# Splitting the first batch's input loads between two issuing engines in an attention and two-MoE kernel

## The chip, the cores and the metric

The kernel runs on one core of a Trainium2 chip. The metric is the device time of one execution in microseconds (us), the median of several runs. One core has five engines with instruction streams of their own: TensorE (PE, matrix multiplications), VectorE (DVE), ScalarE (ACT, activation functions and copies), GpSimd (POOL) and SyncE (SP, which here only issues transfers). Transfers between device memory (HBM) and the on-chip memory (SBUF) are moved by 16 DMA engines, which the issuing engines share. An engine carries out its instructions in program order; a transfer is also an instruction of the engine that issues it, and the instruction waits until the semaphores it names have reached their values.

## The reference, cut to what matters

Three layers in a row. The first is an attention over 32 memory slots per head, for 4 batches of 8 heads and 576 positions with a head size of 64; its output (2304 tokens of 512 numbers) goes through a gated feed-forward layer of 1536, and then through 8 experts of 1024 of which each token takes the best two.

```python
a = softmax(phi, axis=2)                       # phi (4, 8, 576, 32)
k_m = einsum('bhsm,bhsd->bhmd', a, k)          # 32 memory keys per head
v_m = einsum('bhsm,bhsd->bhmd', a, v)
attn = softmax(q @ k_m.T / 8) @ v_m            # (4, 8, 576, 64)
x = attn, heads joined                         # (2304, 512)
x = (silu(x @ w_gate) * (x @ w_val)) @ w_out   # 512 -> 1536 -> 512
logits = x @ g + log1p(exp(x @ n)) * noise     # 8 experts, best two
out = sum over the two of weight * (relu(x @ w1[e]) @ w2[e])
```

## The kernel before

The tokens are worked in 8 blocks of 288, two blocks to a batch, and the 8 heads of a batch in two groups g = 0, 1 that fill the 128 partitions (four heads of 32 slots for phi, 128 rows of positions for keys and values, two heads of 64 for queries). What the change touches is the start of the program, the work of the first batch ahead of block 0.

**The loads.** All loads of this stretch are issued by SP (`Q` in the code; `A` is ACT). `load_phi(0, 0)` and `load_phi(0, 1)` come first (128 partitions by 576 numbers each, 288 KB), then `load_part(0, 0, 0)` (the keys of group 0), `load_q(0)` (the queries of block 0), and the keys of group 1, the values of group 0 and the values of group 1 (each 128 by 1152 numbers, 576 KB). Behind them `load_wa` loads pieces of the first layer's weights, 512 KB each, 16 at once and later ones as `low` frees the places (tiles stg, early, stw, stx).

**The waits of a transfer.** Each transfer that SP or ACT issues signals one of eight semaphores (DMAHW0 to DMAHW7) when it has landed, and these are given out in turn in the order of the program, over both issuing engines together. A transfer therefore waits, before it is issued, for the landing of the one eight places earlier in the program. The seven input loads and the first weight load take the eight semaphores for the first time and wait for nothing.

**The work of the first batch.** For each group: `s1_a` (the maximum of phi over positions, DVE), `s1_e` (the exponential, ACT), `s1_b` (transposes, PE), `s1_bc` (their copy out, ACT, tile en), then `s1_c` (the product with keys or values, PE, tile pkv), `s1_cv`, `s1_d` and `s1_dc` (scaling, transposing and copying into tile km). `s2_first` and `s2_a`, `s2_e`, `s2_b`, `s2_c`, `s2_d` are the scores and the second softmax of block 0 (tiles psc, sm, at, x). `proj_a` multiplies the memory values into the first layer's weights, and `gv(0, f)` are block 0's gate products for the slice f of 1536/12 (tiles pg, pv), `down(0, f)` its output product (tile acc). Before its first exponential ACT loads its function table (line 232, by a first activation on a small tile named warm). `spin(n)` is n matmuls of ones, whose result nobody reads. `top` (ACT) and `low` (DVE) turn each loaded weight piece into 32-bit numbers; `low` frees its place. The queries of block 1 (`load_q(1)`) are issued in block 0's slice 3; their first reader on PE are the score products of block 1 (line 343, tile psc).

Each engine's order is that of these calls, written out by hand; nothing reorders it.

Of the kernel before, what the change touches and what calls it, by code (L numbers as in the profile page):

```python
# [74 lines left out]
def moe_program(ctx, tc, xin, wa, wgn, nz, wb, out):  # L75
# [10 lines left out]
    V, A, P, G, Q = nc.vector, nc.scalar, nc.tensor, nc.gpsimd, nc.sync  # L86
# [28 lines left out]
    PH, KV, QT, RA = {}, {}, {}, {}  # L115
    ROW = 18 * D

    def section(b, name):
        o, n = PLACE[name]
        return xin[b, o:o + 128 * n].rearrange("(p n) -> p n", n=n)  # L120

    def load_phi(b, g):
        t = att.tile([128, S], F32, tag="phi", name="phi", bufs=2)
        Q.dma_start(t, section(b, f"phi{g}"))
        PH[b, g] = t

    def load_part(b, g, s):
        if (b, g) not in KV:
            if b == 0 and g:
                KV[b, g] = wpool.tile([128, 4096], F32, tag="X1", name="kv", bufs=1)[:, :2 * ROW].rearrange(  # L130
                    "p (s w) -> p s w", s=2)
            else:
                KV[b, g] = att.tile([128, 2, ROW], F32, tag="kv", name="kv", bufs=1)
        Q.dma_start(KV[b, g][:, s], section(b, f"{'kv'[s]}{g}"))

    def load_kv(b, g):
        for s in range(2):
            load_part(b, g, s)

    def load_q(i):  # L140
        QT[i] = att.tile([128, 4, BT], F32, tag="q", name="qt", bufs=1)
        Q.dma_start(QT[i], section(i // 2, f"q{i % 2}").rearrange("p (q t) -> p q t", q=4))

    ORDER = [(0, 0), (0, 1), (1, 0), (1, 1)]
    for f in range(NF1):
# [59 lines left out]
    def low(n):  # L205
# [3 lines left out]
        for m in FREES.get(n, ()):  # L209
            load_wa(m)  # L210

    load_phi(0, 0)
    load_phi(0, 1)
    load_part(0, 0, 0)
    load_q(0)
    for g, s in ((1, 0), (0, 1), (1, 1)):
        load_part(0, g, s)
# [500 lines left out]
    for b in range(1, B):  # L718
        i = 2 * b - 2
        n = AT["s1"][min(b, 2)]  # L720
        for g in range(2):
            later(i, 18.5 if b == 1 else -4, load_phi, b, g)
        later(i, 18.5 if b == 1 else -4, load_kv, b, 0)
        later(i, n[5] + 0.06, load_kv, b, 1)
        later(i, n[0], both, s1_a, b)
        later(i, n[1], both, s1_e, b)
        later(i, n[2], both, s1_r, b)
        for g in range(2):
            for m, fn in zip(n[3 + 6 * g:], (s1_b, s1_bc, s1_c, s1_cv, s1_d, s1_dc)):
                later(i, m, fn, b, g)  # L730
        for j, o in enumerate(AT["proj"][b]):
            i, f = 2 * b - 1 + o // NF1, o % NF1
            put(i, 2 * f + 1.95, proj_a, b, j)
            later(i, 2 * f + 2, proj_h, b, j)
            later(i, 2 * f + 2, proj_b, b, j)
    for i in range(1, NB):
        put(i - 1, 6, load_q, i)
        n = AT["s2"].get(i - 1, AT["s2"][2])
        put(i - 1, n[0], s2_p, i)
        put(i - 1, n[1], s2_t, i)  # L740
        put(i - 1, n[2], both, s2_a, i)
        put(i - 1, n[3], both, s2_e, i)
        for g in range(2):
            for m, fn in zip(((n[4], n[5], n[6]), (n[7], n[8], n[9]))[g], (s2_b, s2_c, s2_d)):
                put(i - 1, m, fn, i, g)
# [594 lines left out]
    for p in range(pairs):  # L1340
        e, q = 2 + p // 4, p % 4
# [62 lines left out]
    for p in range(pairs):  # L1404
        e, q = 2 + p // 4, p % 4
# [135 lines left out]
```

## Time and profile before

| | |
|---|---|
| median of 3 runs | 840.27 us (839.26 to 840.96) |
| the profiled execution | 842.7 us, of which the span shown by the profile is 840.9 us |
| PE busy | 824.5 us, 98% of the span |
| DVE, ACT, POOL busy | 636.9, 391.0, 243.8 us |
| moved by DMA | 143.20 MB, 170 GB/s over the span |

Times of rows count from the start of the span. The 1.8 us between the span and the execution's time lie outside the instructions shown. A busy PE is not a PE at its peak, since matmuls overlap and their ends are modelled. PE's busy digit is 7 in the first of the profile's 40 slices (21 us each), 6 in the last and 9 in all others, so the places where PE could be waited out are at the two ends.

### The profile page before, as it was taken

The numbers are of one execution on the slowest core, as the hardware profiler recorded it, in microseconds if no ns is written. First come the engines' busy times: TensorE is split into PE (matmuls) and PEld (weight loads), VectorE is DVE, ScalarE is ACT, GpSimd is POOL, SyncE is SP. The second block draws the span as 40 slices with busy tenths as digits, with TensorE's granted clock in tenths as the row PEclk, the third lists the DMA queues.
The fourth block names the chain that finished last, engine by engine and source line by source line (L and its number), as shares of the span: only waits on it lengthen the run. The fifth ranks groups of instructions, "written<-read, shape, count | busy, mean of one in ns | idle before, by whom it ended". The sixth has DMA issues, their size and how long they took to land.

```text
span 840.9 us, 16644 instructions
## 1 busy us (share of the span) xinstructions
PE 824.5 (98%) x6317; PEld 731.9 (87%) x6317; DVE 636.9 (76%) x1534; ACT 391.0 (47%) x804; POOL 243.8 (29%) x345
## 2 busy tenths in 40 slices
PE   7999999999999999999999999999999999999996
PEld 5777988899999998999999988988888888888885
DVE  5888588766867677777784587898889988899771
ACT  5765565343433334333444545546445454554430
POOL 2000012524333142444123223322415234144242
PEclk9999999999999999999999999999999999999999
DMA  9994748784427373447946993645574654654421
GB/s 349 401 347 138 227 153 303 243 262 134 116 67 217 86 211 84 134 112 176 269 151 204 222 244 73 137 128 114 129 170 100 160 125 102 164 136 113 161 84 64
DMA packets 79145, 143.20 MB, mean 170 GB/s; under 512 B 16176, under 2 KB 36880, under 8 KB 79056
## 3 DMA queue, kind: packets, MB, share of 16 engines
q1 hardware_dynamic: 59696, 100.66, 39.0%
q0 software_dynamic: 19360, 41.38, 20.8%
q8 instruction: 52, 0.85, 0.4%
q14 instruction: 37, 0.30, 0.1%
HBM read 105.34 MB, written 36.68 MB: 169 GB/s over the span
## 4 chain that ended last, share of the span: by engine, by line
PE 81%; DMA 9%; DVE 5%; issue 2%; ACT 1%; SPq 1%; POOL 1%; POOLq 0%; DVEq 0%; ACTq 0%
PE acc L1177 18%; PE ph L1163 17%; PE acc L496 14%; PE pg L463 9%; PE pv L463 7%; PE ph L974 4%; PE acc L992 3%; PE pp L343 2%; DMA wb<-wb 2%; PE acc L492 1%; DMA stx<-wa 1%; DMA out<-pv,ix 1%; DMA kv<-xin 1%; PE pT L518 1%; DMA qt<-xin 1%
## 5 line engine op out<-in xcount | busy, mean ns | idle before, releaser
L1177 PE MATMUL acc<-ws,hs 128*128 128x512 f32 (+1 forms) x690 | 174.9, 394 | 0.0
L1163 PEld LDWEIGHTS ph<-xh,ws 128*128 128x128 f32 x1008 | 151.0, 188 | 9.7 <-ACT y L1200 0.7
L1163 PE MATMUL ph<-xh,ws 128*128 128x308 f32 x1008 | 157.4, 304 | 0.3 <-ACT y L1200 0.3
L1177 PEld LDWEIGHTS acc<-ws,hs 128*128 128x128 f32 (+1 forms) x690 | 122.7, 184 | 24.3
L496 PE MATMUL acc<-a,ro 128*128 128x288 f32 x576 | 116.4, 295 | 0.0
L1017 POOL DMA_INDIRECT out<-pv,ix x40 | 63.1, 1576 | 175.2 <-ACT pv L1009 66.9
L496 PE MATMUL acc<-a,os 128*128 128x288 f32 x432 | 105.8, 294 | 0.0
L463 PE MATMUL pg<-x,pt 128*128 128x288 f32 x576 | 102.3, 311 | 1.9 <-DVE ta L476 0.9
L463 PEld LDWEIGHTS pg<-x,pt 128*128 128x128 f32 x576 | 81.1, 188 | 20.4 <-issue 6.0
L496 PEld LDWEIGHTS acc<-a,ro 128*128 128x128 f32 x576 | 92.2, 188 | 0.0
L463 PE MATMUL pv<-x,pt 128*128 128x288 f32 x576 | 91.9, 295 | 0.0
L463 PEld LDWEIGHTS pv<-x,pt 128*128 128x128 f32 x576 | 81.7, 188 | 0.0
L476 DVE SCALAR_TENSOR_TENSOR ta<-ta,pg 128x288 f32<-128x288 f32 x84 | 37.8, 450 | 57.4 <-ACT ta L471 57.3
L660 POOL DMA_INDIRECT xs<-R,gidx x48 | 47.0, 979 | 110.5 <-DMA xs<-R,gidx 94.3
L496 PEld LDWEIGHTS acc<-a,os 128*128 128x128 f32 x432 | 74.1, 189 | 0.1
L471 ACT ACTIVATE ta<-pg 128x288 f32<-128x288 f32 x84 | 34.3, 408 | 79.7 <-PE pg L463 79.7
L482 ACT ACTIVATE a<-ta 128x288 fp32r<-128x288 f32 x84 | 37.3, 444 | 71.9 <-DVE ta L477 71.7
L453 POOL DMA_DIRECT2D os<-osl x72 | 40.8, 567 | 100.7 <-PE acc L496 58.5
L974 PE MATMUL ph<-xt,wm 128*128 128x384 f32 (+1 forms) x256 | 55.4, 307 | 0.0
L974 PEld LDWEIGHTS ph<-xt,wm 128*128 128x128 f32 x256 | 43.7, 189 | 2.5
L477 DVE TENSOR_TENSOR ta<-ta,pv 128x288 f32<-128x288 f32 x84 | 38.1, 454 | 8.7
L483 DVE TENSOR_TENSOR a<-ta,a 128x288 fp32r<-128x288 f32 x84 | 37.4, 445 | 5.2 <-ACT a L482 4.9
(241 smaller groups left out, 1449.9 us busy)
## 6 DMA issues: line engine op xcount, KB each, us to landing
wb<-wb SPq DMA_DIRECT2D x70, 512.0 KB, 4.3
os<-osl POOLq DMA_DIRECT2D x72, 256.0 KB, 3.4
kv<-xin SPq DMA_DIRECT2D x16, 576.0 KB, 6.9
xl<-xs SPq DMA_DIRECT2D x40, 160.0 KB, 6.5
stg<-wa SPq DMA_DIRECT2D x12, 511.8 KB, 10.4
out<-zt SPq DMA_DIRECT2D x1, 5888.0 KB, 26.0
xd<-R SPq DMA_DIRECT2D x8, 603.0 KB, 5.6
qt<-xin SPq DMA_DIRECT2D x8, 576.0 KB, 7.4
```

Of the source, the lines that this page charges most:

```text
L453: G.dma_start(r(lo), r(osl[f][:, :]))
L463: P.matmul(p, r(PT[f // 2, g][:, w, f % 2, 128 * a:128 * a + 128]), r(X[i][:, s, g, :]), start=(n == 0), stop=(n == 5))
L476: V.scalar_tensor_tensor(ta, ta, 1.0, pg, op0=OP.add, op1=OP.mult)
L477: V.tensor_mul(ta, ta, pv)
L482: A.activation(r(ah[:, 0, :]), ta, AF.Copy)
L483: V.tensor_sub(r(ah[:, 1, :]), ta, ah[:, 0, :])
L496: P.matmul(ACC[i][c], r(OS[i, f][w][:, o]), r(ah[:, s, :]), start=(f == 0 and n == 0), stop=(f == NF1 - 1 and n == 2))
L660: G.indirect_dma_start(out=xs[:, :], out_offset=bass.IndirectOffsetOnAxis(ap=RT[i][:, t, n:n + 1], axis=0), in_=R[i][:, t, :], in_offset=None)
L974: P.matmul(p, r(w[:, c]), r(x[:, k, b, :]), start=(m == 0), stop=(m == 11))
L1017: G.indirect_dma_start(out=out, out_offset=bass.IndirectOffsetOnAxis(ap=IX[e][:h, t:t + 1], axis=0), in_=PV[e, t][:h], in_offset=None, com ...
L1163: P.matmul(out, r(w[i][:, c + 128 * k:c + 128 * k + 128]), r(x[:, m, k, a]), start=(start and n == 0), stop=(n == 5), skip_group_check=not ...
L1177: P.matmul(AC2[e, t][:h], r(a[:, n, o]), r(w[b][:, n]), start=(f == 0 and m == 0), stop=(f == NF2 - 1 and m == 2))
```

## The change

For batch 0 the keys, the values and the queries are each loaded by two transfers of 64 partitions, the lower half issued by SP and the upper half by ACT; of the two loads of phi, group 0's stays on SP and group 1's goes to ACT. Later batches are loaded as before. There are 12 transfers in the place of 7, the six of ACT standing ahead of its table load.

```diff
+    def halves(two, t, src):
+        if two:
+            Q.dma_start(t[:64], src[:64])
+            A.dma_start(t[64:], src[64:])
+        else:
+            Q.dma_start(t, src)
+
     def load_phi(b, g):
         t = att.tile([128, S], F32, tag="phi", name="phi", bufs=2)
-        Q.dma_start(t, section(b, f"phi{g}"))
+        if b == 0:
+            (A if g else Q).dma_start(t, section(b, f"phi{g}"))
+        else:
+            Q.dma_start(t, section(b, f"phi{g}"))
...
-        Q.dma_start(KV[b, g][:, s], section(b, f"{'kv'[s]}{g}"))
+        halves(b == 0, KV[b, g][:, s], section(b, f"{'kv'[s]}{g}"))
...
-        Q.dma_start(QT[i], section(i // 2, f"q{i % 2}").rearrange("p (q t) -> p q t", q=4))
+        halves(i == 0, QT[i], section(i // 2, f"q{i % 2}").rearrange("p (q t) -> p q t", q=4))
```

SP's first instructions before, with the semaphores each waits for (kv_98 holds keys and values of group 0, kv_102 those of group 1, stg the first weight pieces):

```order
L124 DMA phi_94<-xin 128x576
L124 DMA phi_96<-xin 128x576
L134 DMA kv_98<-xin 128x1152
L142 DMA qt_100<-xin 128x1152
L134 DMA kv_102<-xin 128x1152
L134 DMA kv_98<-xin 128x1152
L134 DMA kv_102<-xin 128x1152
L176 DMA stg_106<-wa 128x2047
L176 DMA stg_108<-wa 128x2047 [waits DMAHW0_49]
L176 DMA stg_110<-wa 128x2047 [waits DMAHW1_49]
L176 DMA stg_112<-wa 128x2047 [waits DMAHW2_49]
```

All input loads are issued without a wait, and the fourth weight load is the one that waits for the keys of group 0 (DMAHW2). The same place on SP now (kv_104 is group 1's tile):

```order
L132 DMA phi_94<-xin 128x576
L124 DMA kv_98<-xin 64x1152
L124 DMA qt_101<-xin 64x1152
L124 DMA kv_104<-xin 64x1152
L124 DMA kv_98<-xin 64x1152 [waits DMAHW0_49]
L124 DMA kv_104<-xin 64x1152 [waits DMAHW2_49]
L186 DMA stg_111<-wa 128x2047 [waits DMAHW4_49]
L186 DMA stg_113<-wa 128x2047 [waits DMAHW5_49]
L186 DMA stg_115<-wa 128x2047 [waits DMAHW6_49]
L186 DMA stg_117<-wa 128x2047 [waits DMAHW7_49]
```

With more transfers in the same round of eight semaphores, the halves of the values wait for landings, and every weight load does. ACT's first instructions before:

```order
L232 ACT_TABLE_LOAD
L232 ACTIVATE warm_143<-warm_143 128x1 [waits Pool_49]
L272 ACTIVATE phi_94,st_170<-phi_94,st_170 128x576 [waits DMAHW0_49,DVE_49]
L272 ACTIVATE phi_96,st_172<-phi_96,st_172 128x576 [waits DMAHW1_49,DVE_49]
L294 ACTIVATE en_219<-pT_211 128x512 [waits PE_49]
```

The table load was the first of them. Now:

```order
L132 DMA phi_96<-xin 128x576
L125 DMA kv_98<-xin 64x1152
L125 DMA qt_101<-xin 64x1152
L125 DMA kv_104<-xin 64x1152
L125 DMA kv_98<-xin 64x1152 [waits DMAHW1_49]
L125 DMA kv_104<-xin 64x1152 [waits DMAHW3_49]
L242 ACT_TABLE_LOAD
L242 ACTIVATE warm_148<-warm_148 128x1 [waits Pool_49]
L282 ACTIVATE phi_94,st_175<-phi_94,st_175 128x576 [waits DMAHW0_49,DVE_49]
L282 ACTIVATE phi_96,st_177<-phi_96,st_177 128x576 [waits DVE_49]
```

Six transfers stand ahead of the table load on ACT. The fifth waits for the landing of phi of group 1 (DMAHW1), the sixth for that of the upper half of the keys of group 0 (DMAHW3, the second row).

## Rows read from the trace of the kernel before

**Rows 1.** The page: PE's busy time, and the DMA share by slice
```profile
PE 824.5 (98%) x6317; PEld 731.9 (87%) x6317; DVE 636.9 (76%) x1534; ACT 391.0 (47%) x804; POOL 243.8 (29%) x345
...
DMA  9994748784427373447946993645574654654421
```

**Rows 2.** Busy time in two stretches: engines, granted clock, DMA share, GB/s
```profile
0.00:5.00 5.00, 3.38 (x30) 3.12 (x30) 1.53 (x4) 1.87 (x3) 4.41 (x17) 1.00 0.59 204
5.00:10.00 5.00, 3.99 (x56) 3.35 (x57) 1.01 (x6) 2.77 (x8) 0.63 (x1) 1.00 0.98 358
```

**Rows 3.** Timeline of SP's transfers: start, us, what
```profile
0.76 0.86 SPq L124 DMA_DIRECT2D phi<-xin  x2
...
8.71 0.33 SPq L176 DMA_DIRECT2D stg<-wa  x1
...
40.80 0.33 SPq L142 DMA_DIRECT2D qt<-xin  x1
```

**Rows 4.** Tiles phi and kv in the first 30 us: issue and landing
```profile
DMA to landing us min/median/max: 3.0/3.2/3.3
...
L134 SPq DMA_DIRECT2D kv<-xin x4: 424/436/1617, 1.7 to 3.6; - x4
...
DMA to landing us min/median/max: 7.0/9.4/10.9
```

**Rows 5.** Timeline of ACT, idle time before and what ended it in brackets
```profile
0.76 1.28 ACT L232 ACT_TABLE_LOAD   x1 [0.76 <-PEq L1533]
...
4.62 0.77 ACT L272 ACTIVATE phi<-phi,st 128x576 f32<-128x576 f32 x1 [2.36 <-DVE st L267]
...
17.04 0.79 ACT L203 ACTIVATE top<-stg 128x512 f16<-128x512 bf16 x1
...
31.32 0.79 ACT L203 ACTIVATE top<-stw 128x512 f16<-128x512 bf16 x1 [1.61 <-DMA stw<-wa]
```

**Rows 6.** Timeline of DVE
```profile
16.46 0.46 DVE L368 TENSOR_TENSOR sm<-sm,rd 128x288 f32<-128x288 f32 x1
...
17.87 0.69 DVE L207 SCALAR_TENSOR_TENSOR wa<-stg,top 128x512 int32<-128x512 int32 x1 [0.35 <-ACT top L203]
...
32.15 0.69 DVE L207 SCALAR_TENSOR_TENSOR wa<-stw,top 128x512 int32<-128x512 int32 x1 [1.07 <-ACT top L203]
```

**Rows 7.** Timeline of PE
```profile
5.54 1.11 PE L285 MATMUL pT<-ident,phi 128*128 128x128 f32 x4 [1.14 <-ACT phi L272]
...
8.83 1.03 PE L307 MATMUL pkv<-kv,en 128*32 128x64 f32 x40 [0.47 <-ACT en L295]
...
28.73 2.21 PE L492 MATMUL acc<-a,ro 128*128 128x288 f32 x8 [0.86 <-DVE ro L207]
...
34.17 1.08 PE L463 MATMUL pg<-x,pt 128*128 128x288 f32 x6
...
35.98 0.66 PE L343 MATMUL pp<-wa,km 64*32 64x256 f32 x16
...
37.39 2.21 PE L492 MATMUL acc<-a,ro 128*128 128x288 f32 x8
...
39.22 0.64 PE L463 MATMUL pg<-x,pt 128*128 128x288 f32 x2
...
41.65 2.10 PE L492 MATMUL acc<-a,ro 128*128 128x288 f32 x8
...
45.26 1.09 PE L343 MATMUL pp<-wa,km 64*32 64x256 f32 x32
46.29 2.21 PE L492 MATMUL acc<-a,ro 128*128 128x288 f32 x8
...
51.19 0.72 PE L343 MATMUL psc<-qt,km 64*32 64x288 f32 x16 [1.11 <-DMA qt<-xin]
...
77.19 0.60 PE L285 MATMUL pT<-ident,phi 128*128 128x128 f32 x4
```

## The prediction

> **What bounds the kernel now.** The page comes first: PE is busy for 824.5 of 840.9 us [rows 1], so a change to the loads of the first batch can move the time only where PE waits near the start. The second view is the busy time by stretch. The DMA engines reach a share of 0.59 in the first 5 us and 0.98 in the next five [rows 2], and the page's DMA digits read 9 for the first three slices, 63 us [rows 1]: from about 5 us on, the transfers run at the rate of the DMA engines and not at that of the engine that issues them. The third view is the timelines of ACT, DVE and PE over the first 55 us. Two things run side by side there. One is a chain of computation: phi lands, its exponential starts on ACT at 4.62 [rows 5], then transposes and the first product with the keys on PE at 8.83 [rows 7], the second softmax on DVE [rows 6], and PE's first output product at 28.73, for which PE waited 0.86 us on DVE [rows 7]. The other is the stream of weight loads, which ACT meets at 31.32, after 1.61 us of idle time that a landing ended [rows 5], and which PE meets at 51.19, where it had waited 1.11 us for the queries of block 1 [rows 7]. So the stream sets the time up to 51.19, and the chain has room against it that I work out below.
>
> **What the change adds and removes on the issue side.** SP has six input transfers in place of seven and ACT six in place of none. A transfer of SP takes 0.42 to 0.44 us of its sequencer, with one of 1.62 [rows 4]. No row shows one on ACT, nor one of 64 partitions: from below it could be nearly free, from above 1.62; I take 0.43, the usual value, as a rate that does not depend on the size of the tile. The bytes stay the same. What an earlier issue can win is time in which the DMA engines stand idle after the first issue: 0.41 of the first 5 us, 2.05 us, less the 0.76 us before any issue [rows 2, 3], so at most 1.3 us.
>
> [...]
>
> **What the change adds on ACT.** The six transfers stand ahead of ACT's table load. Four need no wait; the fifth waits for phi of group 1 and the sixth for the upper half of group 0's keys. ACT goes in order, so behind these two waits stand the table load, both exponentials of phi, and with them the whole chain of computation. Phi landed 3.0 to 3.3 us after its issue [rows 4], near 4 us, so the fifth costs nothing beyond the sixth. The sixth decides. In the kernel before, the fourth weight load waits on the keys of group 0 and starts at 8.71 [rows 3]; that is their landing, and it agrees with 7.0 us, the shortest time from issue to landing of the four [rows 4]. That is the upper end. The lower end is a landing in the order of issue at the rate that the DMA engines ran: phi and these keys are 2 x 288 + 576 KB, 1.18 MB; 204 GB/s over 5 us are 1.02 MB, and the rest at 358 GB/s takes another 0.45 us [rows 2], so 5.5 us. I take 7.6, two thirds of the way to the upper end: that row is the direct one and the same bytes stand ahead, but the issue comes about 0.45 us earlier and less stands behind.
>
> Then ACT issues the last half (0.43), loads its table (1.28 [rows 5]) and runs the small first activation. Before, the table load started at 0.76 and ACT was idle again 2.36 us ahead of 4.62, at 2.26 [rows 5], so both take 1.50 us. The exponential starts at 7.6 + 0.43 + 1.50 and some 0.07 of gaps, 9.6. Against 4.62 that is 5.0 us late; by the ends of the landing 2.9 (exponential at 7.5) and 6.1 (10.7).
>
> **How much of it reaches the end.** Step by step along the chain:
> - PE had waited 0.47 us before the key product at 8.83 [rows 7], just behind the landing at 8.71. Late transposes use that up: minus 0.47.
> - The score products and the value products find their data landed; DVE's second softmax follows at the same distance. At 17.87 DVE had waited 0.35 us for ACT's second `top` [rows 6], which ACT began at 17.04, 0.12 us after DVE had finished its subtraction at 16.92 [rows 5, 6]. With the chain late, both weight pieces have landed and the `top` work is done ahead: minus 0.35. From there to 31 us DVE's row of work has no gap, so the rest passes on in full: 5.0 - 0.82 = 4.2 us at PE's output product of 28.73.
> - From there PE's own waits are waits for the stream. One pair of products before a projection takes 1.81 us (34.17 to 35.98), the next takes 2.43 (39.22 to 41.65): 0.62 lost. One double projection takes 1.41 (35.98 to 37.39), a later one 1.03 (45.26 to 46.29): 0.38 lost. At 51.19 it is 1.11 [rows 7]. Together 2.1 us, which a late PE does not wait. ACT and DVE can fall back on their idle 1.61 and 1.07 us [rows 5, 6] and what follows.
> - The weight loads themselves do not get late with the chain: each waits for a landing eight places earlier, and the places they need had been freed long before. That holds the queries of block 1, issued at 40.80 [rows 3], at their place.
> - After 51.19 PE is at 98% and more and gives nothing back.
>
> So the chain costs 4.2 - 2.1 = 2.1 us; with the ends of the landing 0.0 (2.9 - 0.82 - 2.1) and 3.2. The profiled execution took 842.7 us, a span of 840.9 and 1.8 outside it; the sum against it is 844.8. The median of the runs lies 2.4 us under the profiled execution, and the forecast goes from the median: 840.3 + 2.1 = 842.4. A measurement of this kernel tells about 0.2% from no change, 1.7 us.
>
> **The rivals.**
> First, the stream covers all of it: the keys land near 5.5 us, because in the kernel before it was the transfers queued behind them that held them up, and now fewer stand there. Then the chain is 2.1 us late at 28.73 and the three waits absorb it: no change, between -0.4 and +1.0 us. For it: the rate of the DMA engines allows it. Against it: 7.0 us for the shortest landing.
> Second, and on the other side, the earlier issue leads. Two sequencers fill the DMA engines sooner, every later transfer lands up to 1.3 us earlier, the queries of block 1 with them, and PE's waits at 35 to 51 us shrink. This decides only from the point where ACT is released so early that the chain stays under the waits, with the keys' landing near 5.5: 840.3 - 1.3 = 839.0. For it: 0.59 of share in the first stretch. Against it: the first bytes cannot come sooner than phi's first issue, which stays where it is, and the same late exponential takes away what it wins.
> [...]
> [...]
>
> **How the numbers follow.** The forecast (842.4, own range 841.3 to 843.5, from landings at 6.5 and 8.7) has 0.45; the covered case 0.30; the leading stream 0.08; the clock 0.17. Slower by over 0.2% holds about 0.7 of the forecast and all of the clock case but a little, and a bit of the covered case: 0.51. Within 0.2% is most of the rest, 0.44. Faster by over 0.2% would need more than the 1.3 us that the stream can win: 0.05. The range is 839.6 to 844.8: down into the leading stream's case, up over the clock's.
>
> **What would show it.** Right: ACT's table load starts at 7 to 9 us in place of 0.76, just behind its sixth transfer, and the first exponential between 9 and 10.7; PE's idle time ahead of the transposes is 5 us longer; PE's wait for the queries of block 1 is gone. Wrong: a table load before 6 us (then the landing was the mis-sized term and the time stays); the queries' landing more than 1 us away from 51; idle time of PE at a weight wait after 52 us; or transposes and key products at a different speed than in rows 7.

## The result

The changed kernel is slower: 847.13 us (median of 6 runs, 845.39 to 849.08) against 840.81 for the kernel before (6 runs), a ratio of 1.0076 with an interval of 1.0064 to 1.0087. The forecast had the direction and gave 842.4, with an upper end of 844.8. Five single executions among the runs below took over 1000 us; the ratios and their intervals leave these out, the medians do not.

The profiled execution of the changed kernel took 845.39 us. Its page, the rows that answer to [rows 1] and the span:

```profile
span 843.6 us, 16654 instructions
...
PE 822.9 (98%) x6317; PEld 732.4 (87%) x6317; DVE 636.2 (75%) x1534; ACT 390.5 (46%) x804; POOL 243.7 (29%) x345
...
DMA  9993838884427364447846993645564654654421
```

No engine is busier than before by more than 0.5 us (PEld) and the DMA engines are as busy in the first three slices; the time went into waiting. What ACT did at the start, as [rows 5] (ACTq are the transfers that ACT issues):

```profile
1.21 0.55 ACTq L125 DMA_DIRECT2D kv<-xin  x1
...
2.42 6.32 ACTq L125 DMA_DIRECT2D kv<-xin  x3
8.77 1.28 ACT L242 ACT_TABLE_LOAD   x1 [8.77 <-DMA kv<-xin]
10.06 0.20 ACT L242 ACTIVATE warm<-warm 128x1 f32<-128x1 f32 x1
10.17 0.76 ACT L282 ACTIVATE phi<-phi,st 128x576 f32<-128x576 f32 x1
```

The table load starts at 8.77 in place of 0.76, right behind the sixth transfer, and the exponential at 10.17 in place of 4.62. The busy time by stretch, as [rows 2], with the two stretches that follow (the last two columns are the DMA share and GB/s):

```profile
0.00:5.00 5.00, 3.38 (x30) 3.12 (x30) 0.43 (x3) 0.00 (x0) 4.41 (x17) 1.00 0.62 183
5.00:10.00 5.00, 0.00 (x0) 0.00 (x0) 1.35 (x2) 1.23 (x1) 0.63 (x1) 0.81 1.02 271
10.00:15.00 5.00, 3.92 (x52) 3.33 (x52) 0.63 (x4) 3.30 (x10) 0.00 (x0) 0.51 1.04 259
15.00:20.00 5.00, 4.84 (x129) 2.85 (x125) 2.61 (x8) 2.05 (x5) 0.00 (x0) 1.00 1.02 363
```

This is what the forecast had not seen: from 5 to 15 us the DMA engines have a share of 1.02 and 1.04 and move 271 and 259 GB/s. The first of them had 358 before [rows 2]; the second was this:

```profile
10.00:15.00 5.00, 4.85 (x139) 2.93 (x138) 2.84 (x8) 1.30 (x4) 0.00 (x0) 1.00 1.02 412
```

The engines are full and slow. PE of the changed kernel, as [rows 7]:

```profile
11.07 1.11 PE L295 MATMUL pT<-ident,phi 128*128 128x128 f32 x4 [6.67 <-ACT phi L282]
...
13.83 1.33 PE L317 MATMUL pkv<-kv,en 128*32 128x64 f32 x40
...
33.83 2.21 PE L502 MATMUL acc<-a,ro 128*128 128x288 f32 x8 [0.86 <-DVE ro L217]
...
54.10 0.72 PE L353 MATMUL psc<-qt,km 64*32 64x288 f32 x16
```

PE is 5.1 us late at its first output product (28.73 before) and 2.9 at the score products of block 1 (51.19 before), where it no longer waits for the queries. The key product takes 1.33 us in place of 1.03. Set against the first trace of before, that reads like the forecast. But the median moved by 6.3 us, and these two executions stand only 2.7 us apart: the first trace of before is of an execution 1.9 us over its median, this one is 1.7 us under. The experiments had to find out which of the two comparisons is usual.

### The profile page after: what moved, and what is told of

It is laid out like the page before. It is cut to its first block, busy times and chain, and to the rows that moved or that the text cites. A ratio compares the mean times of both kernels' runs of the same rounds, so it can differ in the third digit from the quotient of the medians.

```text
span 843.6 us, 16654 instructions
## 1 busy us (share of the span) xinstructions
PE 822.9 (98%) x6317; PEld 732.4 (87%) x6317; DVE 636.2 (75%) x1534; ACT 390.5 (46%) x804; POOL 243.7 (29%) x345
## 4 chain that ended last, share of the span: by engine, by line
PE 89%; DVE 5%; DMA 2%; issue 2%; ACT 1%; ACTq 0%; POOL 0%; POOLq 0%; DVEq 0%
PE acc L1187 18%; PE ph L1173 17%; PE acc L506 14%; PE pg L473 9%; PE pv L473 8%; PE acc L1002 7%; PE ph L984 7%; PE acc L502 3%; PE pp L353 3%; PE pkv L317 1%; DMA out<-pv,ix 1%; PE pT L528 1%; DMA kv<-xin 1%; PE psc L353 1%; PE plg L539 1%
```

## The experiments

All times are medians with the ratio to the kernel before, of the same chip and session. A ratio's interval is the 95% one.

| run | us | before | ratio and interval |
|---|---|---|---|
| after_again | 845.96 | 839.98 | 1.0058 (1.0035 to 1.0082) |
| sp_halves | 846.92 | 839.98 | 1.0074 (1.0050 to 1.0097) |
| act_four | 842.69 | 839.98 | 1.0029 (1.0012 to 1.0046) |
| hold | 844.00 | 839.98 | 1.0042 (1.0027 to 1.0057) |
| sp_even_odd | 841.84 | 840.72 | 1.0018 (1.0006 to 1.0030) |
| even_odd | 844.32 | 840.72 | 1.0046 (1.0030 to 1.0062) |
| two_whole | 840.31 | 840.72 | 0.9988 (0.9970 to 1.0006) |
| four_even_odd | 840.62 | 840.13 | 1.0005 (0.9994 to 1.0017) |
| hold_spin | 842.90 | 840.13 | 1.0028 (1.0017 to 1.0039) |
| two_whole_b | 841.43 | 840.13 | 1.0017 (1.0002 to 1.0031) |
| late_values | 846.60 | 840.38 | 1.0075 (1.0063 to 1.0087) |
| after_c | 846.24 | 840.38 | 1.0070 (1.0057 to 1.0082) |
| even_odd_c | 843.55 | 840.38 | 1.0044 (1.0027 to 1.0061) |
| hold_c | 843.78 | 840.38 | 1.0045 (1.0032 to 1.0058) |

**The changed kernel again** (after_again, no edit).

> The changed kernel once more, for a second trace and more times. Three theories of the 6.3 us. Hold: ACT waits for the upper half of group 0's keys, the chain of computation is late, and PE is late by 5 us at its first output product. Stream: the halves on two queues are moved slower (the first trace of the changed kernel has 271 and 259 GB/s from 5 to 15 us, before 358 and 412), so the weights and the queries of block 1 land about 2 us late. Clock: PE's idle 6.7 us ahead of the transposes cost it the full clock for a stretch. All three expect about 847 here. Hold expects the table load near 8.8 again; stream expects the queries of block 1 to be issued near 43 in place of 40.8, later in a slower run; clock expects the low stretch to differ between runs and the slower runs to have the lower mean clock.

845.96. The table load starts at 7.27 here, not near 8.8, and the rates are 259 and 258 GB/s from 5 to 15 us: the slow stream is a property of the kernel and not of one execution. The queries of block 1 are issued at 43.20, as the stream theory expected.

**The halves without the hold** (sp_halves).

```diff
-            A.dma_start(t[64:], src[64:])
+            Q.dma_start(t[64:], src[64:])
...
-            (A if g else Q).dma_start(t, section(b, f"phi{g}"))
+            Q.dma_start(t, section(b, f"phi{g}"))
```

> The same halves, but all 13 transfers issued by SP; ACT issues none and loads its table at 0.76 as before. Hold: nothing is left, 840.8 within 1 us. Stream by two queues: one queue moves them at the old rate, 358 GB/s from 5 to 10 us, 840.8 within 1. Stream by halves (smaller transfers are slower, or 13 transfers in one round of eight semaphores starve the engines): the rate stays near 270 and the time is 842 to 844. Clock: 840.8.

846.92: as slow as the changed kernel, although ACT loads its table at 0.76 and starts its exponential at 4.62. The rates:

```profile
5.00:10.00 5.00, 3.79 (x55) 2.76 (x56) 1.37 (x6) 2.77 (x8) 0.63 (x1) 0.72 0.99 226
10.00:15.00 5.00, 3.18 (x64) 2.09 (x63) 1.61 (x4) 0.59 (x3) 0.00 (x0) 0.84 1.04 233
15.00:20.00 5.00, 3.80 (x76) 2.23 (x75) 3.16 (x8) 0.60 (x3) 0.00 (x0) 0.50 1.02 279
```

The time is above the 842 to 844 that was expected if the halves are slow. PE waits three times for keys and values:

```profile
13.54 1.02 PE L317 MATMUL pkv<-kv,en 128*32 128x64 f32 x40 [1.77 <-DMA kv<-xin]
...
16.09 1.34 PE L317 MATMUL pkv<-kv,en 128*32 128x64 f32 x36 [0.56 <-DMA kv<-xin]
...
19.12 0.86 PE L317 MATMUL pkv<-kv,en 128*32 128x64 f32 x24 [0.62 <-DMA kv<-xin]
```

Besides these 2.95 us, its granted clock, the third number from the end of a row above, is 0.50 from 15 to 20 us, and 0.50 again from 20 to 25. So hold alone falls as the whole cause, and two queues fall as the reason of the slow stream: one queue is slower still, at a full share of the DMA engines. Left were the size of the transfers, the eight semaphores, and which partitions a half covers.

**Four transfers on ACT, none waiting** (act_four; the values whole, from SP).

```diff
-        halves(b == 0, KV[b, g][:, s], section(b, f"{'kv'[s]}{g}"))
+        halves(b == 0 and s == 0, KV[b, g][:, s], section(b, f"{'kv'[s]}{g}"))
```

> Phi, keys and queries as in the changed kernel, but the values whole, from SP: ACT issues only the four transfers that wait for nothing and loads its table near 3 us. Hold: the exponential of phi starts near 5 and the time is 840.8 within 1. Stream: the transfers of the two queues are still slow up to 10 us, the stream is 1 to 2 us late, 842 to 843. Clock: PE idles little, 840.8.

842.69. ACT's exponential starts at 5.87, the rate from 5 to 10 us is 254 GB/s. As the stream theory had it; the halves of neighbouring partitions that are left are those of the keys and the queries.

**The hold without the halves** (hold; the loads of before, all from SP).

```diff
     A.activation(warm, warm, AF.Exp)
+    hold = const.tile([128, 1], F32, name="hold")
+    A.activation(hold, QT[0][:, 0, 0:1], AF.Copy)
```

> The kernel before with its loads untouched, and one small activation on ACT, behind the table load, that reads the queries of block 0: ACT's first exponential is held until about 10.4, as late as in the changed kernel, while the transfers stay as they were. Hold with the absorption that was predicted: 2.1 to 3.2 us, 843 to 844. Hold as the whole cause: 846 to 847. Stream: the stream is on time, so 843 to 844. Clock: PE idles as long as in the changed kernel, so its share shows here too; with the clock as the main cause 845 to 847.

844.00, at the upper end of what the forecast's absorption allowed. The rates are those of before:

```profile
8.95 0.20 ACT L234 ACTIVATE hold<-qt 128x1 f32<-128x1 f32 x1 [6.69 <-DMA qt<-xin]
9.06 0.76 ACT L274 ACTIVATE phi<-phi,st 128x576 f32<-128x576 f32 x1
```

```profile
5.00:10.00 5.00, 0.04 (x1) 0.04 (x1) 0.44 (x2) 1.05 (x4) 0.63 (x1) 0.84 0.98 373
10.00:15.00 5.00, 5.00 (x60) 4.10 (x61) 0.86 (x5) 2.20 (x6) 0.00 (x0) 0.50 1.02 417
```

The first exponential was held to 9.06 only, since the queries landed earlier than in the first trace, and yet the loss is about 3.5 to 4 us. The absorption was in doubt.

**A second trace of the kernel before** (before_again, no edit).

> The kernel before once more, for a second trace. Its first trace is of an execution of 842.7 us, 2 us over the median of its runs. If that execution had a late stream of its own, the queries of block 1 are issued 2 to 3 us earlier here than 40.8, PE waits under 0.5 us for them at its score products of block 1, and the room of 2.1 us that the prediction found there is smaller in a usual execution: the 6 us are then hold plus stream with little absorbed. If not, this trace reads like the first and the missing 3 us arise elsewhere.

One execution of 840.66 us, span 838.9, so a usual one. Its SP issues the queries of block 1 at 39.12, 1.7 us earlier than in the first trace. Here are its rates from 5 to 15 us, and PE's rows behind them:

```profile
5.00:10.00 5.00, 3.03 (x58) 2.29 (x59) 0.95 (x6) 2.46 (x8) 0.63 (x1) 1.00 0.97 351
10.00:15.00 5.00, 4.92 (x93) 3.08 (x92) 2.40 (x7) 1.19 (x4) 0.00 (x0) 0.56 1.02 414
```

```profile
8.58 0.90 PE L307 MATMUL pkv<-kv,en 128*32 128x64 f32 x40 [1.70 <-DMA kv<-xin]
...
29.09 2.21 PE L492 MATMUL acc<-a,ro 128*128 128x288 f32 x8 [0.86 <-DVE ro L207]
...
50.01 0.72 PE L343 MATMUL psc<-qt,km 64*32 64x288 f32 x16 [0.58 <-DMA qt<-xin]
```

From the first output product to the score products PE takes 20.92 us here, 22.46 in the first trace [rows 7], and 20.27 in the changed kernel (33.83 to 54.10), which does not wait there. What a late PE can win back in this stretch is thus 0.65 us in a usual execution of before, and 2.2 in the one that the forecast read. That execution had a late stream of its own, with the queries issued at 40.80 [rows 3].

**Halves of another shape, one queue** (sp_even_odd; sp_halves with even and odd partitions).

```diff
-            Q.dma_start(t[:64], src[:64])
-            Q.dma_start(t[64:], src[64:])
+            Q.dma_start(t[0:128:2], src[0:128:2])
+            Q.dma_start(t[1:128:2], src[1:128:2])
```

> All 13 transfers from SP as in the run of halves on SP (846.9), but a half is the even or the odd partitions of the tile, not the lower or the upper 64. Size, number of transfers, issue times and waits are the same. If a half is slow because it covers only 64 neighbouring partitions, the rate from 5 to 15 us goes from 226 and 233 GB/s back to 350 or more and the time to 840.5 to 842. If it is slow because it is small, or because 13 transfers share eight semaphores, rate and time stay: 846 to 848.

841.84 in place of 846.92, and the rates are back, the first of them a little under the expected 350:

```profile
5.00:10.00 5.00, 4.66 (x60) 3.81 (x61) 0.98 (x6) 2.56 (x8) 0.63 (x1) 1.00 0.95 338
10.00:15.00 5.00, 4.57 (x134) 2.69 (x132) 3.08 (x8) 1.33 (x5) 0.00 (x0) 1.00 1.02 404
15.00:20.00 5.00, 2.91 (x52) 1.94 (x52) 3.59 (x10) 3.67 (x9) 0.00 (x0) 1.00 1.02 415
```

Only the set of partitions differs between the two kernels, and with it the rows of the source in HBM that fill them; the number, the size, the issuing engine and the waits of the transfers are the same. This settles that the slow stream comes from halves of 64 neighbouring rows, and from neither the size, the number nor the semaphores of the transfers. Whether it is the partitions or the source rows no run separates. A ratio of 1.0018 is left for 12 transfers in place of 7, whose issue takes 0.6 us for a half (the 13 in some of the expectations is a miscount; it is 12 in every kernel whose keys, queries and values are all halved).

**Halves of another shape, two queues** (even_odd; the same edit in the changed kernel, the odd half from ACT).

> The changed kernel with even and odd partitions in place of lower and upper: two queues, the same waits on ACT ahead of its table load. If neighbouring partitions are the cause of the slow stream, the rate is back at 350 or more, what is left is ACT's hold, and the time is that of the held kernel before, 843 to 844.5; the table load may come some tenths earlier. If two queues are slow by themselves: 845 to 847, as the changed kernel.

844.32, the time of the held kernel before. ACT's table load starts at 7.54, the rates are 365 and 405 GB/s. The profiled execution, 845.41, is one of its slower ones: its first output product comes at 34.82 and its score products of block 1 at 55.09. A faster trace of the same kernel follows below.

**Whole transfers on two queues** (two_whole).

```diff
-        Q.dma_start(t, section(b, f"phi{g}"))
+        (A if b == 0 and g else Q).dma_start(t, section(b, f"phi{g}"))
...
-        Q.dma_start(KV[b, g][:, s], section(b, f"{'kv'[s]}{g}"))
+        (A if b == 0 and (g, s) == (0, 1) else Q).dma_start(KV[b, g][:, s], section(b, f"{'kv'[s]}{g}"))
...
-        Q.dma_start(QT[i], section(i // 2, f"q{i % 2}").rearrange("p (q t) -> p q t", q=4))
+        (A if i == 0 else Q).dma_start(QT[i], section(i // 2, f"q{i % 2}").rearrange("p (q t) -> p q t", q=4))
```

> The kernel before with its seven whole transfers of 128 partitions shared out: phi of group 1, the queries and the values of group 0 from ACT, the rest from SP; none of ACT's three waits, and its table load starts near 2.1. Second queue harmless: the rates of before, exponential at 4.6 to 5, 839.5 to 841. Earlier issue helps: up to 1.3 us less, 838.7. Second queue slow: rate under 300 GB/s from 5 to 10 us and 842 or more.

840.31, not told apart from before. The stream gains what the second rival hoped for:

```profile
5.00:10.00 5.00, 3.58 (x53) 2.71 (x54) 1.76 (x6) 3.14 (x8) 0.63 (x1) 0.73 1.02 418
```

418 GB/s, and the queries of block 1 are issued at 38.39 in place of 39.12. But the two loads of phi are now issued at the same time, at 0.76, the exponential behind them starts at 5.50 in place of 4.33 in the second trace of before, and PE comes to its score products at 50.35 without a wait, where the second trace of before had 50.01 with one: the chain takes back what the stream gives.

**Neither hold nor neighbouring halves** (four_even_odd; act_four with even and odd partitions).

> Two queues with even and odd partitions, and ACT issues only the four transfers that wait for nothing (the values whole, from SP): neither the hold nor the slow stream. If these two are the whole loss: 840.7 within 1, the exponential of phi near 5.5, the rate from 5 to 10 us at 350 or more. If the second queue or the split costs on its own: 842 to 843, as the same with lower and upper halves (842.7).

840.62, ratio 1.0005: nothing is left of the loss, with the keys and the queries still split over two queues. The exponential starts at 5.85, the rate from 5 to 10 us is 397 GB/s.

**The clock's part of the hold** (hold_spin; the held kernel before with a longer opening spin).

```diff
-    spin(30)
+    spin(100)
```

> The kernel before with ACT held on the queries of block 0, and an opening spin of 100 matmuls in place of 30, so that PE is busy until about 9 us and does not idle ahead of the transposes. If the low clock behind that idle time is part of the hold's 4 us: the four transposes take 0.6 us in place of 1.11, the chain is about 1 to 2 us shorter and the time 842 to 843. If the clock plays no part: 844.0 within 0.7, as the held kernel.

842.90, ratio 1.0028, against 1.0042 and 1.0045 of the held kernel; the intervals overlap. With the longer spin the first four transposes take 0.66 us and the second four 1.04, and the granted clock from 10 to 15 us is 0.67, against 0.50 and 0.51 in two traces of the held kernel:

```profile
10.77 0.66 PE L287 MATMUL pT<-ident,phi 128*128 128x128 f32 x4 [2.20 <-ACT phi L274]
...
11.53 1.04 PE L287 MATMUL pT<-ident,phi 128*128 128x128 f32 x4
```

From the exponential to the first output product the trace takes 22.89 us (9.87 to 32.76), against 23.51 and 23.64 in the two of the held kernel. So the longer spin is worth about 1 us by the medians and 0.6 to 0.75 by the traces; the intervals do not tell it from nothing. The granted clock from 20 us on is another matter, to which the last runs come.

**Another sharing out of whole transfers** (two_whole_b; group 0's keys, the queries and group 0's values from ACT, edited as two_whole).

> The kernel before with whole transfers: both phi, group 1's keys and values and the weights from SP, group 0's keys, the queries and group 0's values from ACT, none of them waiting, ACT's table load near 2.2. Earlier issue helps the stream: the queries of block 1 are issued 0.5 to 1 us before 39.1 and the time is 839.5 to 840.5. The chain sets the time: exponential near 4.5 as before, keys landed sooner, 839 to 840. The second queue disturbs: 841 or more.

841.43, ratio 1.0017: slower, as expected for a second queue that disturbs. ACT's exponential starts at 6.02 and not near 4.5, and the earlier stream (queries issued at 38.39) does not make up for it. That phi is late because the keys are now issued beside it is the likely reason, not a measured one.

**A third trace of before** (before_third, no edit).

> A third trace of the kernel before. If the first one was the unusual one: the queries of block 1 issued near 39.1 and PE waits 0.3 to 0.8 us for them. If the room varies from execution to execution: anything between 0.3 and 1.2 us.

In this execution PE was granted 0.85 of its clock from about 9 us on, and the time was 894.56 us, so only its transfers can be read: the queries of block 1 are issued at 39.09, as in the second trace. Two of three have it near 39.1; the first trace is the odd one.

**Four kernels on one chip.** What was open was how the loss divides. The new one here (late_values) issues the upper halves of the values from ACT behind its copies:

```diff
-        halves(b == 0, KV[b, g][:, s], section(b, f"{'kv'[s]}{g}"))
+        if b == 0 and s:
+            src = section(b, f"v{g}")
+            Q.dma_start(KV[b, g][:64, s], src[:64])
+            LATER.append((KV[b, g][64:, s], src[64:]))
+        else:
+            halves(b == 0, KV[b, g][:, s], section(b, f"k{g}" if not s else f"v{g}"))
...
+    for t, src in LATER:
+        A.dma_start(t, src)
+    for n in range(len(HOMES)):
+        load_wa(n)
```

(The last four lines stand behind the copies of `s1_bc`; the loop over `load_wa` moved there.)

> The changed kernel, but ACT issues the upper halves of the values only behind its two exponentials and the copies that follow, and the first weight loads stand behind them in the order of the program: every first-batch transfer is still a lower or an upper half, ACT's table load is near 3. If the hold is the larger part and the stream adds 1 to 2.5 us: 842 to 843.5. If the stream alone is worth as much as the whole: 845 to 847.

> The changed kernel beside the other three: 6 us over the kernel before, within 1.

> The changed kernel with even and odd partitions: if the stream adds to the hold, 1 to 2.5 us under the changed kernel; if the hold covers the stream, the same as the changed kernel within 0.7.

> The held kernel before, with the loads of before: the same as the even and odd form within 0.7 if the hold is all that is left there; more than 1 us below it if two queues or 13 transfers cost on their own.

846.24 for the changed kernel, 843.55 for its even and odd form, 843.78 for the held kernel before, 840.38 for before. By these medians the held kernel loses 3.4 us (its interval is 2.7 to 4.9), and the changed kernel another 2.7 against its even and odd form, a little more than the 1 to 2.5 expected; the intervals of these two touch (1.0057 to 1.0082, 1.0027 to 1.0061), but in all three sessions the changed kernel is 5.9 to 6.3 us over before, and its even and odd form 3.2 to 3.6 in two. The even and odd form and the held kernel are 0.2 us apart, as expected. The first exponential on ACT, PE's first output product and its score products of block 1 in the three, in this order:

```profile
9.85 0.76 ACT L282 ACTIVATE phi<-phi,st 128x576 f32<-128x576 f32 x1
...
35.47 2.21 PE L502 MATMUL acc<-a,ro 128*128 128x288 f32 x8 [0.86 <-DVE ro L217]
...
55.74 0.71 PE L353 MATMUL psc<-qt,km 64*32 64x288 f32 x16
```

```profile
8.72 0.76 ACT L282 ACTIVATE phi<-phi,st 128x576 f32<-128x576 f32 x1
...
32.30 0.99 PE L502 MATMUL acc<-a,ro 128*128 128x288 f32 x3 [0.86 <-DVE ro L217]
...
52.58 0.72 PE L353 MATMUL psc<-qt,km 64*32 64x288 f32 x16
```

```profile
8.35 0.76 ACT L274 ACTIVATE phi<-phi,st 128x576 f32<-128x576 f32 x1
...
31.99 1.24 PE L494 MATMUL acc<-a,ro 128*128 128x288 f32 x4 [0.85 <-DVE ro L207]
...
52.28 0.71 PE L345 MATMUL psc<-qt,km 64*32 64x288 f32 x16
```

All three take 20.27 to 20.29 us from the one to the other, so none waits for the stream; against the second trace of before (29.09 and 50.01) they are 6.4, 3.2 and 2.9 us late at the first place, and 5.7, 2.6 and 2.3 at the second. From the score products to the end of the span the changed kernel takes 789.4 us, the even and odd form 788.5, the held kernel 789.2 and before 788.9: the loss is made ahead of the score products.

These rows also say how the halves come in, since PE itself waits for none of their landings in the changed kernel, where it waited for three in the run of halves on SP. The first way is the hold itself: in two of three traces the upper half of the keys, for which ACT waits, lands later, and the exponential starts at 10.17, 8.68 and 9.85 in the changed kernel against 8.94 and 8.72 in two traces of the even and odd form. The second is PE's clock. From the exponential to the first output product the held kernel takes 23.51 and 23.64 us, the faster even and odd trace 23.58 and the first trace of the changed kernel 23.66, all with a granted clock of 1.00 from 20 to 25 us. The other two traces of the changed kernel take 25.80 and 25.62, and the slower even and odd trace 25.88, 2.0 to 2.3 us more. Their granted clock in that stretch is lower: 0.71 in after_again. These are the rows of after_c, of the slower and, for comparison, of the faster even and odd trace (the clock is the third number from the end):

```profile
20.00:25.00 5.00, 2.90 (x59) 2.47 (x57) 4.37 (x11) 2.17 (x7) 0.00 (x0) 0.80 1.01 407
```

```profile
20.00:25.00 5.00, 3.76 (x45) 2.85 (x52) 3.99 (x10) 1.84 (x6) 0.00 (x0) 0.57 1.02 407
```

```profile
20.00:25.00 5.00, 4.07 (x71) 3.10 (x72) 4.61 (x12) 3.25 (x9) 0.00 (x0) 1.00 1.03 409
```

The same 14 matmuls of a spin, at 23.30, 22.19 and 21.41, take 1.70, 1.70 and 0.94 us. Ahead of it PE stands idle for 2.10, 1.90 and 1.83 us inside its value product, with nothing in the profile that released it. So of the 3.2 us between after_c and the faster even and odd trace at the first output product, 1.1 is the later exponential and 2.0 lies behind it, where the clock differs. The 2.7 us are thus what the set of partitions costs by the medians; how they divide between a longer hold and an execution's clock is not shown, nor why the clock falls in one execution and not in the next.

late_values separates nothing. Its 846.60 lies in the range expected if the stream alone is the whole, but for another reason: ACT issues the values' halves only at 10.51, behind the first weight loads of SP, which start at 8.04, and PE waits for them:

```profile
14.39 0.33 PE L340 MATMUL pT<-ident,kz 128*128 128x128 f32 x1
20.29 1.34 PE L322 MATMUL pkv<-kv,en 128*32 128x64 f32 x36 [5.57 <-DMA kv<-xin]
```

It says only that the chain without the hold was near its time until 14.7 us (this transpose is at 13.64 in the second trace of before) and then lost 5.57 us to one late landing.

## Why the prediction was wrong

**The hold: right.** The table load behind the sixth transfer, the exponential 5 us late (forecast at 9.6; 10.17, 8.68 and 9.85 in three traces, 4.1 to 5.6 us behind 4.62), a lost wait for the queries of block 1: all seen. The landing of the keys' upper half, behind which the sixth transfer starts at 6.8 to 8.3, was between the bounds. Of the 0.82 us taken off ahead of the first output product only the 0.47 is seen: from the first transposes to the key product the two first traces take 3.29 us before and 2.76 after, but from there to the first output product 19.90 and 20.00.

**The absorption: mis-sized, and taken from the wrong execution.** The step "Together 2.1 us, which a late PE does not wait" is true of the execution it was read from, as 22.46 us against 20.27 show. In a usual execution it is 0.65. The forecast then took this sum, which belongs to an execution of 842.7 us, and put it on the median of 840.3. Had it stayed with its own execution it would have been 844.8, near the profiled 845.39. Part of the chain's room was larger than forecast in return: PE waited 1.70 us for the keys at 8.58 in the second trace, not 0.47. The held kernel gives the net size, with a hold of 4.0 to 4.7 us against the 4.33 of that trace: 3.4 us and a ratio of 1.0032 to 1.0058 in place of 2.1 us.

**"The bytes stay the same": the term that was missing.** The forecast priced the split itself at nothing, and bounded the stream by what an earlier issue could win. It took a transfer of 64 partitions to run at the rate of one of 128. From 5 to 10 us the runs show 226 to 271 GB/s for halves of neighbouring partitions, 338 to 397 for even and odd ones and 332 to 422 for whole tiles, at the same nearly full share of the DMA engines (0.95 to 1.04), and 2.7 us of time on top of the hold. With it fell the step that kept the weight stream and the queries of block 1 at their place: they are issued at 42.96 to 43.49 in the changed kernel, at 37.91 and 38.80 in the held and the even and odd one. Their landing, by an estimate from these issue times and the 10.3 us that they took to land in the first trace of before, comes at 53.3 to 53.8 in the changed kernel, the sign of being wrong that the forecast had named (over 1 us from 51); PE comes later still, at 54.10 and 55.74 in two traces, and does not wait for it. The issue time was taken as 0.43 whatever the size; it is 0.56 to 0.85 us on SP and 0.53 to 0.62 on ACT for a half that waits for nothing.

From 5 to 10 and from 10 to 15 us, lower and upper halves from one queue move at 226 and 233 GB/s in place of 351 and 414 in the second trace of before, 0.64 and 0.56 of it. With lower and upper halves from two queues in flight together, 249 to 271 is a little more. Why halves of neighbouring rows are slower is not shown; the runs show only that the set of partitions, or of the source rows with it, decides.

**The rivals.** The stream covering all of it did not happen in any run with a held ACT. The leading stream is real in two_whole (418 GB/s), but buys no time. The clock has 0.17 in the forecast and stands under the upper end of its range; that PE's products are slowed because PE stands idle ahead of the transposes, the cost taken for it, no run shows. From 5 to 10 us PE does nothing in the first trace of the changed kernel and in after_c alike, and from 10 to 15 us its granted clock is 0.51 in the one and 1.00 in the other, with a key product of 1.33 and of 1.45 us. One sign of being wrong that the forecast had named was seen in that: 1.33 to 1.45 us for the key product of the changed kernel in place of 1.03 [rows 7]. The transposes alone decide little: four take 1.11 us in the first traces of before and of the changed kernel, 0.66 in the second trace of before, and a spin with which the first four took 0.66 bought about 1 us within the noise. What the runs showed in its place comes later: where the granted clock from 20 to 25 us was 0.57 to 0.80 and not 1.00, the way to the first output product took 2.0 to 2.3 us more, in two of three traces of the changed kernel and in one of two of its even and odd form.

**What stays open.** Why the first trace of before had a late stream, why PE stands idle for 1.0 to 2.2 us inside its value product in most of the traces, and what decides whether its clock falls behind that. No version beat the kernel before beyond its interval; two_whole, at 0.9988 with an upper end of 1.0006, is the nearest.

## What to carry to other kernels

Where a computing engine issues transfers, count the semaphores that each waits for and what stands behind: here ACT's table load started at 8.77 in place of 0.76, right behind its sixth transfer, and in the held kernel a wait of about that length ahead of the first exponential cost 3.4 us. If a tile must be loaded in two parts, try interleaved partitions beside halves of the tile; here, from 5 to 10 us, they moved at 338 to 397 GB/s and the halves at 226 to 271. Read waiting time that a delay could use up in more than one execution, and put the sum on the execution it was read from.

## What the runs showed of the hardware

From 5 to 10 us, lower and upper halves of 64 partitions were moved at 226 to 271 GB/s where even and odd halves of the same size were moved at 338 to 397, at a DMA share of 0.95 to 1.02 in both. A transfer of 64 partitions was not cheaper to issue than one of 128: 0.56 to 0.61 us on SP for the first of them, against 0.43, where SP alone issues. PE's granted clock differed between executions of one kernel: 0.57 and 1.00 from 20 to 25 us in two traces of the even and odd form, with 25.88 and 23.58 us from the exponential to the first output product. The first microseconds varied between executions of the same kernel: the queries of block 1 were issued at 39.09, 39.12 and 40.80 in three traces of the kernel before.
